# Reordering the first loads, tile 3's transposes and PE's idle matmuls in a fused linear attention and SwiGLU kernel

## The chip, the cores and the metric

The kernel runs on one core of a Trainium2 chip. The metric is the device time of one execution in microseconds (us). The engines are called as in the profile: PE (TensorE, matmuls; PEld is its weight load), DVE (VectorE), ACT (ScalarE), POOL (GpSimd) and SP (SyncE, which here only issues DMAs). ACT issues DMAs too. Each engine works through its own list of instructions in program order.

## The reference

`x` is 2048 x 512, in bf16, as are all weights.

```python
def phi(t): return where(t > 0, t + 1, exp(t)) + 1e-6

xn = layernorm(x)                       # over the last axis, no scale or shift
q, k, v = split(xn @ wqkv)              # 32 heads of 16
kv  = einsum("bhsd,bhse->bhde", phi(k), v)
z   = phi(k).sum over s
o   = (phi(q) @ kv) / (phi(q) . z + 1e-6)
A   = o @ wo
B   = (silu(xn @ w_gate) * (xn @ w_up)) @ w_down     # 512 -> 1792 -> 512
out = x + A + B
```

## The kernel before

`x` is cut into 16 tiles of 128 rows; tile t lies in `x_sb[:, t, :]` with one row in each partition. The program is written out by hand as calls like `stat(4)` or `kproj(2)`. Each call appends instructions to the lists of the engines that it uses. A small class `_Prog` remembers who wrote and who reads each named resource (`("x", t)`, `("xnT", t)`, `("bank", i)`, ...) and adds the semaphore waits. So the order of calls is the order of work on every engine, and an instruction that waits holds up all that stands behind it on its engine. A DMA that waits holds up its issuing engine's queue in the same way.

The steps of a tile t are:

- `stat(t)`: mean and variance on DVE (`bn_stats`, L275; `bn_aggr`, L278), then the reciprocal root of the variance on POOL (L294, L301). For tile 0 the addition of 1e-5 (L294) is on DVE.
- `xn(t)` or `xn_dve(t)`: the normalized tile `xn_sb`, on DVE (L283). Tile 0 is done in two halves of columns (`xn_half`, L326).
- The transpose of `xn_sb` into `xnT`: for tiles 0 to 2 four matmuls against an identity on PE and a copy out of PSUM on ACT (`transpose_half` L338 and L347, `transpose_pe` L310 and L317), for later tiles a DMA on SP's queue (`transpose_dma`, L354).
- `kproj(t)` and `qproj(t)`: four matmuls of 512 columns each (L363; `proj_half` L376 for K of tile 0), into PSUM banks `kb(t)` = 0 or 2 and `qb(t)` = 1 or 3.
- `exp_k(t)` and `exp_q(t)` on ACT (L399, L405, L409), then `feat_k(t)` on DVE (clip L416, maximum and addition L425), which also puts the running sum of phi(k) on POOL (`zsum`, L446 and L450).
- `gtacc(t)`: four matmuls (L458) that add the transpose of xn times phi(k) into banks 4 to 7, over all tiles. Until then the transposes on PE use banks 4 to 7.

After the 16 tiles comes a long part in which PE is fed from `xnT`: the FFN's gate and up matmuls (`ffn_mm`, L550), the small matrices of the attention (L648, L671), and the output tiles (L722, L733, with the addition of `x` at L746). This part is the same before and after.

The first loads are issued on two queues, SP's and ACT's: x tiles, then the columns of `wqkv` for K ("wk") and for Q ("wq"), each in two parts of 256 KB, one on each queue (`wqkv_load`, L202). x tiles 4 to 15 are loaded by SP in four DMAs, of which the first waits for x 0 and x 1 (`xload`, L195). `fill` (L247) puts matmuls without use for the result on PE while it has no other work. They multiply a tile of zeros, `idle`, which DVE sets at the start (L241).

In the loop over tiles, tables give which later tiles get their `stat` (STAT) and their `xn` (XN) in iteration t, and `wpiece` issues the parts of `w_gate` and `w_up` on SP's queue.

Of the kernel before, what the change touches and what calls it, by code (L numbers as in the profile page):

```python
# [10 lines left out]
P = 128  # L11
# [3 lines left out]
NT = S // P  # L15
# [93 lines left out]
def bass_parallel_sum__linear_attn_block__swiglu_ffn__prompt_kernel(  # L109
# [12 lines left out]
    K = _Prog()  # L122
    pe, act, dve, pool, sp = nc.tensor, nc.scalar, nc.vector, nc.gpsimd, nc.sync
    bf, f32 = dt.bfloat16, dt.float32

    with contextlib.ExitStack() as es:
        E = es.enter_context

        def sb(name, shape, d=bf):
            return E(nc.sbuf_tensor(name, [P] + shape, d))  # L130

        x_sb = sb("x_sb", [NT, D])
# [4 lines left out]
        wg_sb = sb("wg_sb", [NDC, F])  # L137
# [5 lines left out]
        stats = sb("stats", [NT, 6], f32)  # L143
        mv = sb("mv", [NT, 2], f32)
        vpe = sb("vpe", [NT], f32)
        rstd = sb("rstd", [NT], f32)
# [2 lines left out]
        ek = sb("ek", [NE, D])  # L149
        eq = sb("eq", [NT, D])  # L150
        warm = sb("warm", [1], f32)
        idle = sb("idle", [512])
        pkq = sb("pkq", [NT, 2, D])
        zacc = sb("zacc", [D], f32)
        zhi = sb("zhi", [D])
# [19 lines left out]
        banks = [psum[:, i, :] for i in range(8)]  # L175
# [10 lines left out]
        def bk(i):  # L186
            return ("bank", i)


        xv = xin.rearrange("(p t) d -> p t d", t=NT)  # L190
        ov = oview.rearrange("(p t) d -> p t d", t=NT)

        def xload(eng, h, t0, n, after=()):
            K.dma(
                eng, lambda: h.dma_start(x_sb[:, t0:t0 + n, :], xv[:, t0:t0 + n, :]),  # L195
                r=list(after), w=[("x", t0 + i) for i in range(n)],
            )

        def wqkv_load(eng, h, name, i, c0, n):
            K.dma(  # L200
                eng,
                lambda: h.dma_start(  # L202
                    wqkv_sb[:, c0:c0 + n, i * D:(i + 1) * D],
                    A_wqkv[c0 * P:(c0 + n) * P, i * D:(i + 1) * D].rearrange("(c p) f -> p c f", p=P),
                ),
                w=[(name, c0)],
            )
# [4 lines left out]
        def wpiece(name, dst, src, c):  # L212
            K.dma("sp", lambda: sp.dma_start(dst[:, c, :], src[c * P:(c + 1) * P, :]), w=[(name, c)])

        xload("sp", sp, 0, 1)
        xload("act", act, 1, 1)
        wqkv_load("sp", sp, "wk", 1, 0, 2)
        wqkv_load("act", act, "wk", 1, 2, 2)
        xload("sp", sp, 2, 1)
        xload("act", act, 3, 1)  # L220
        wqkv_load("sp", sp, "wq", 0, 0, 2)
        wqkv_load("act", act, "wq", 0, 2, 2)
        xload("sp", sp, 4, 2, [("x", 0), ("x", 1)])
        xload("sp", sp, 6, 4)
        xload("sp", sp, 10, 2)
        xload("sp", sp, 12, 4)

# [10 lines left out]
            r=[("ident",)], w=[("ident",)],  # L238
        )
        K.op("pool", lambda: pool.memset(nhalf[:, :], -0.5), w=[("nhalf",)])  # L240
        K.op("dve", lambda: dve.memset(idle[:, :], 0.0), w=[("idle",)])  # L241

        def fill(n, after):
            K.op(
                "pe",
                [
                    (lambda: pe.matmul(banks[3], idle[:, 0:P], idle[:, :], start=True, stop=True))  # L247
                    for _ in range(n)
                ],
                r=[("idle",)] + after, w=[bk(3)],  # L250
            )

        def masks():
# [18 lines left out]


        def bns(t):
            K.op("dve", lambda: dve.bn_stats(stats[:, t, :], x_sb[:, t, :]), r=[("x", t)], w=[("st", t)])  # L275

        def agg(t):
            K.op("dve", lambda: dve.bn_aggr(mv[:, t, :], stats[:, t, :]), r=[("st", t)], w=[("mv", t)])  # L278
# [1 line left out]
        def xn_dve(t):  # L280
            K.op(
                "dve",
                lambda: dve.tensor_scalar(  # L283
                    out=xn_sb[:, t, :], in0=x_sb[:, t, :], scalar1=mv[:, t, 0:1], scalar2=rstd[:, t:t + 1],
                    op0=ALU.subtract, op1=ALU.mult,
                ),
                r=[("x", t), ("mv", t), ("rstd", t)], w=[("xn", t)],
            )
# [16 lines left out]
        def transpose_pe(t, b):  # L305
            tb = banks[b].bitcast(bf)[:, 0:512].rearrange("p (c s) -> p c s", c=NDC)
            K.op(
                "pe",
                [
                    (lambda c=c: pe.transpose(tb[:, c, :], xn_sb[:, t, c * P:(c + 1) * P], ident[:, :]))  # L310
                    for c in range(NDC)
                ],
                r=[("xn", t), ("ident",)], w=[bk(b)],
            )
            K.op(
                "act",
                lambda: act.activation(xnT[:, :, t * P:(t + 1) * P], tb, ACT.Copy),  # L317
                r=[bk(b)], w=[("xnT", t)],
            )
# [52 lines left out]
        def proj_half(t, b, lo, wname, h):  # L372
            K.op(
                "pe",
                [
                    (lambda c=c: pe.matmul(  # L376
                        banks[b], xnT[:, c, t * P:(t + 1) * P], wqkv_sb[:, c, lo:lo + D],
                        start=(c == 0), stop=(c == NDC - 1),
                    ))
                    for c in (2 * h, 2 * h + 1)  # L380
                ],
                r=[("xnTh", t, h), (wname, 2 * h)], w=[bk(b)],
            )

        def kb(t):
            return 2 * (t % 2)
# [4 lines left out]
        def kproj(t):  # L391
            proj(t, kb(t), D, "wk")

        def qproj(t):
            proj(t, qb(t), 0, "wq")

        def exp_k(t):
            K.op(
                "act", lambda: act.activation(ek[:, t % NE, :], banks[kb(t)], ACT.Exp),  # L399
                r=[bk(kb(t))], w=[("ek", t % NE)],  # L400
            )

        def exp_q(t):
            K.op(
                "act", lambda: act.activation(eq[:, t, :], banks[qb(t)], ACT.Exp),  # L405
                r=[bk(qb(t))], w=[("eq", t)],
            )
            K.op(
                "act", lambda: act.activation(pkq[:, t, 1, :], banks[qb(t)], ACT.Copy),  # L409
                r=[bk(qb(t))], w=[("pq", t)],  # L410
            )
# [19 lines left out]
        def feat_k(t):  # L431
            e = t % NE
            clip(ek[:, e, :], ("ek", e))
            if t >= 1:
                zsum(t - 1, e)
            maxadd(pkq[:, t, 0, :], banks[kb(t)], ek[:, e, :], [bk(kb(t)), ("ek", e)], [("pk", t)])
# [17 lines left out]
        def gtacc(t):  # L454
            K.op(
                "pe",
                [
                    (lambda c=c: pe.matmul(  # L458
                        banks[4 + c], xn_sb[:, t, c * P:(c + 1) * P], pkq[:, t, 0, :],
                        start=(t == 0), stop=(t == NT - 1),  # L460
                    ))
                    for c in range(NDC)
                ],
                r=[("xn", t), ("pk", t)], w=[bk(4 + c) for c in range(NDC)],
            )

        def stat(t):
            bns(t)
            agg(t)
            rstd_pow(t)  # L470

        def xn(t):
            xn_dve(t)
            if t >= 3:
                transpose_dma(t)

        stat(0)
        stat(1)
        xn_half(0, 0)
        xn_half(0, 1)  # L480
        xn_dve(1)
        stat(2)
        stat(3)
        xn_dve(2)

        fill(10, [])
        fill(1, [("mv", 0)])
        fill(1, [("rstd", 0)])
        transpose_half(0, 4, 0)
        transpose_half(0, 5, 1)  # L490
        fill(1, [])
        proj_half(0, kb(0), D, "wk", 0)
        proj_half(0, kb(0), D, "wk", 1)
        exp_k(0)
        transpose_pe(1, 6)
        qproj(0)
        exp_q(0)
        transpose_pe(2, 7)
        kproj(1)
        qproj(1)  # L500
        feat_k(0)
        xn(3)

        STAT = {0: (4, 5), 1: (6,), 2: (7,), 3: (8,), 4: (9, 10), 5: (11,), 6: (12,), 7: (13,), 8: (14, 15)}
        XN = {0: (4,), 1: (5,), 2: (6,), 3: (7,), 4: (8,), 5: (9, 10), 6: (11,), 7: (12,), 8: (13,), 9: (14, 15)}

        for t in range(NT):
            if t >= 2:
                kproj(t)
            if t >= 1:  # L510
                exp_k(t)
            if t >= 2:
                qproj(t)
            if t >= 1:
                exp_q(t)
                feat_k(t)
            for i in STAT.get(t, ()):
                stat(i)
            for i in XN.get(t, ()):
                xn(i)  # L520
            if t in (2, 4, 6, 8):
                wpiece("wg", wg_sb, B_w_gate, t // 2 - 1)
            if t == 11:
                for c in range(NDC):
                    wpiece("wu", wu_sb, B_w_up, c)
                wqkv_load("sp", sp, "wv", 2, 0, 4)
                wload("sp", sp, "wo", wo_sb, A_wo)
            if t == 14:
                wload("sp", sp, "wd", wd_sb, B_w_down)
            if t == 12:  # L530
                masks()
            if t >= 2:
                gtacc(t - 2)
        zsum(NT - 1, None)
        gtacc(NT - 2)
# [292 lines left out]
```

## Time and profile before

| | |
|---|---|
| runs | 214.15, 214.5, 215.22 us; median 214.5 |
| the profiled execution | 214.34 us |
| its span (first to last instruction) | 213.0 us |
| PE busy | 207.5 us, 97% of the span |
| DVE, ACT, POOL busy | 119.4, 67.6 and 72.6 us |
| granted TensorE clock, mean of the span | 1.00 |
| a matmul of 512 columns behind another, from 10 us on | 0.216 us |
| FFN's first matmul (L550) in the chain of waits | 49.94 us |

Times in the profile are microseconds from the first instruction. The execution's time is 1.34 us longer than its span. In the timeline a row gives the start, the busy time, engine, line, operation, output and inputs, the count, and in brackets how long the engine sat idle before it and what released it. The duration of one matmul record is its latency (379 ns for 512 columns in a dense stretch); matmuls overlap, so the distance between their starts is what PE needs for one. The granted clock of the page is 1.00 throughout, also in the first microseconds, in which matmuls of 512 columns follow one another at 0.43 us.

### The profile page before, as it was taken

How to read it: one execution, taken by the hardware profiler on the slowest of the kernel's cores; microseconds unless marked ns; L12 is line 12 of the kernel's file. 1: busy time of each engine (PE TensorE's matmuls, PEld its weight loads, DVE VectorE, ACT ScalarE, POOL GpSimd, SP SyncE). 2: the span in 40 equal slices, each digit the busy share in tenths (PEclk: the TensorE clock that was granted, in tenths of full speed). 3: DMA queues.
4: the chain of work that ended last, by engine and by line, in shares of the span. 5: the costliest groups of instructions: out<-in, count | busy, mean ns of one | idle time of the engine just before them, and what ended most of it. 6: DMA issues, size and time to landing. Idle time of an engine off the chain costs nothing.

```text
span 213.0 us, 2744 instructions
## 1 busy us (share of the span) xinstructions
PE 207.5 (97%) x972; PEld 96.0 (45%) x991; DVE 119.4 (56%) x241; ACT 67.6 (32%) x117; POOL 72.6 (34%) x95
## 2 busy tenths in 40 slices
PE   7899999999999999999999999999999999999995
PEld 2344444444544444444444444444444444444454
DVE  2899997333544776446373746464556536364121
ACT  2576666667353332213122302112032213121000
POOL 1559996646013444032130442131414131221100
PEclk9999999999999999999999999999999999999999
DMA  5924598899102011110101011101011010110201
GB/s 188 388 65 125 139 143 207 287 368 266 26 0 52 0 25 25 49 24 28 31 20 49 3 35 39 49 0 49 3 49 25 25 25 28 49 25 26 51 28 51
DMA packets 26671, 16.32 MB, mean 77 GB/s; under 512 B 18592, under 2 KB 25120, under 8 KB 26656
## 3 DMA queue, kind: packets, MB, share of 16 engines
q1 hardware_dynamic: 25824, 15.34, 27.1%
q10 hardware_dynamic: 832, 0.79, 1.2%
q8 instruction: 8, 0.13, 0.3%
q14 instruction: 7, 0.06, 0.1%
HBM read 9.70 MB, written 2.10 MB: 55 GB/s over the span
## 4 chain that ended last, share of the span: by engine, by line
PE 94%; DVE 2%; DMA 2%; issue 1%; POOL 1%; DVEq 0%
PE psum L550 45%; PE psum L733 23%; PE psum L363 12%; PE psum L722 6%; PE psum L458 6%; DMA x_sb<-in_A_x_dram 2%; DVE stats L275 1%; POOL rstd L301 1%; PE psum L648 0%; PE psum L671 0%; DVE xn_sb L283 0%; DVE mv L278 0%; POOL vpe L294 0%; DVE out_sb L746 0%; PE psum L310 0%
## 5 line engine op out<-in xcount | busy, mean ns | idle before, releaser
L565 ACT ACTIVATE sg<-psum 128x512 bf16<-128x512 f32 x56 | 33.4, 598 | 106.8 <-PE psum L550 106.0
L550 PE MATMUL psum<-xnT,wu_sb 128*128 128x512 bf16 x222 | 57.4, 379 | 0.1
L550 PE MATMUL psum<-xnT,wg_sb 128*128 128x512 bf16 x217 | 56.0, 379 | 0.4
L680 POOL TENSOR_TENSOR prod<-pkq,zb 128x512 f32<-128x512 bf16 x16 | 18.6, 1161 | 57.8 <-DVE pkq L425 57.8
L550 PEld LDWEIGHTS psum<-xnT,wu_sb 128*128 128x128 bf16 x224 | 21.9, 98 | 26.4
L550 PEld LDWEIGHTS psum<-xnT,wg_sb 128*128 128x128 bf16 x224 | 21.9, 98 | 26.2
L746 DVE TENSOR_TENSOR out_sb<-psum,x_sb 128x512 bf16<-128x512 f32 (+1 forms) x17 | 11.2, 660 | 36.1 <-PE psum L733 36.1
L571 DVE TENSOR_TENSOR pkq<-psum,sg 128x512 bf16<-128x512 f32 x28 | 19.1, 686 | 18.6 <-PE psum L550 14.1
L704 POOL TENSOR_TENSOR pqn<-pkq,rden 128x512 bf16<-128x512 bf16 x16 | 16.9, 1055 | 36.6 <-DVE rden L698 36.6
L363 PE MATMUL psum<-wqkv_sb,xnT 128*128 128x512 bf16 x122 | 29.0, 379 | 0.3
L571 DVE TENSOR_TENSOR xn_sb<-psum,sg 128x512 bf16<-128x512 f32 x28 | 18.8, 671 | 14.2 <-PE psum L550 13.6
L733 PE MATMUL psum<-wd_sb,xn_sb 128*128 128x512 bf16 (+1 forms) x124 | 25.6, 355 | 0.1
L733 PE MATMUL psum<-wd_sb,pkq 128*128 128x512 bf16 x110 | 25.4, 379 | 0.1
L450 POOL TENSOR_TENSOR zacc<-zacc,pkq 128x512 f32<-128x512 f32 x15 | 17.3, 1153 | 6.9 <-DVE ek L416 6.8
L363 PEld LDWEIGHTS psum<-wqkv_sb,xnT 128*128 128x128 bf16 x124 | 12.0, 98 | 14.5 <-DMA wqkv_sb<-in_A_wqkv_dram 0.3
L733 PEld LDWEIGHTS psum<-wd_sb,xn_sb 128*128 128x128 bf16 x126 | 12.3, 98 | 11.9
L733 PEld LDWEIGHTS psum<-wd_sb,pkq 128*128 128x128 bf16 x112 | 11.0, 98 | 13.2
L722 PE MATMUL psum<-m_sb,eq 128*128 128x512 bf16 (+1 forms) x66 | 16.2, 366 | 0.1
L458 PE MATMUL psum<-pkq,xn_sb 128*128 128x512 bf16 x62 | 15.8, 379 | 0.1
L688 DVE TENSOR_REDUCE den<-prod 128x32 f32<-128x512 f32 x16 | 10.9, 683 | 5.7 <-POOL prod L680 5.7
L399 ACT ACTIVATE ek<-psum 128x512 bf16<-128x512 f32 x16 | 9.6, 598 | 9.9 <-DVE ek L416 2.8
L275 DVE BATCH_NORM_STATS2 stats<-x_sb 128x6 f32<-128x512 bf16 x16 | 10.9, 679 | 2.9 <-DMA x_sb<-in_A_x_dram 2.9
(57 smaller groups left out, 128.4 us busy)
## 6 DMA issues: line engine op xcount, KB each, us to landing
out_dram<-out_sb SPq DMA_DIRECT2D x15, 128.0 KB, 1.7
wg_sb<-in_B_w_gate_dram SPq DMA_DIRECT2D x4, 448.0 KB, 3.8
wu_sb<-in_B_w_up_dram SPq DMA_DIRECT2D x4, 448.0 KB, 4.8
wd_sb<-in_B_w_down_dram SPq DMA_DIRECT2D x1, 1792.0 KB, 13.6
x_sb<-in_A_x_dram SPq DMA_DIRECT2D x2, 512.0 KB, 6.4
wqkv_sb<-in_A_wqkv_dram ACTq DMA_DIRECT2D x2, 256.0 KB, 4.9
wqkv_sb<-in_A_wqkv_dram SPq DMA_DIRECT2D x2, 256.0 KB, 5.2
x_sb<-in_A_x_dram SPq DMA_DIRECT2D x2, 256.0 KB, 5.6
```

Of the source, the lines that this page charges most:

```text
L275: K.op("dve", lambda: dve.bn_stats(stats[:, t, :], x_sb[:, t, :]), r=[("x", t)], w=[("st", t)])
L363: (lambda c=c: pe.matmul(banks[b], xnT[:, c, t * P:(t + 1) * P], wqkv_sb[:, c, lo:lo + D], start=(c == 0), stop=(c == NDC - 1),))
L450: lambda: pool.tensor_tensor(out=zacc[:, :], in0=zacc[:, :], in1=pk, op=ALU.add),
L458: (lambda c=c: pe.matmul(banks[4 + c], xn_sb[:, t, c * P:(c + 1) * P], pkq[:, t, 0, :], start=(t == 0), stop=(t == NT - 1),))
L550: (lambda c=c: pe.matmul(banks[b], w_sb[:, c, fc * P:(fc + 1) * P], xnT[:, c, C * 512:(C + 1) * 512], start=(c == 0), stop=(c == NDC - 1),))
L565: lambda: act.activation(sg[:, j % NSG, :], banks[gb], ACT.Silu),
L571: lambda: dve.tensor_tensor(out=hT(C, fc), in0=banks[ub], in1=sg[:, j % NSG, :], op=ALU.mult,),
L680: lambda: pool.tensor_tensor(out=p, in0=pkq[:, t, 1, :], in1=zb[:, :], op=ALU.mult),
L704: lambda: pool.tensor_tensor(out=pqn[:, t % NPN, :].rearrange("p (h e) -> p h e", e=DH), in0=pkq[:, t, 1, :].rearrange("p (h e) -> p h e", ...
L722: (lambda g=g: pe.matmul(dst, pqnT(t)[:, g, :], m_sb[:, g, lo:hi], start=(g == 0), stop=False,))
L733: (lambda fc=fc: pe.matmul(dst, hT(C, fc)[:, jj * P:(jj + 1) * P], wd_sb[:, fc, lo:hi], start=False, stop=(fc == NFC - 1),))
L746: lambda: dve.tensor_tensor(out=o, in0=src, in1=x_sb[:, t, lo:hi], op=ALU.add),
```

## The change

- x tiles 0 and 1 are loaded in two parts of 64 rows each, one on each queue; both queues start with tile 0.
- x 2 stays on SP between wk and wq. On ACT, wq's part now goes ahead of x 3. x 4 and 5 wait for both parts of wk (instead of x 0 and 1), x 6 to 9 for both parts of wq; x 10 to 15 follow on the same queue.
- Tile 3 is transposed on PE (bank 4) instead of by a DMA. `kproj(1)` goes ahead of tile 2's transposes, `exp_k(0)` behind tile 1's, and tiles 2 and 3 are written out with their own order of `stat`, `xn`, `feat_k` and `gtacc`.
- In the loop a tile's `xn` stands ahead of the next `stat`, both tables change, and the four parts of `w_gate` are issued in iterations 5, 7, 9 and 10 instead of 2, 4, 6 and 8.
- The idle matmuls read constants of 1.0 that the program holds anyway, so DVE's memset goes. They no longer wait for anything; ten have 512 columns and six have 128.

```diff
-        idle = sb("idle", [512])
...
-        xload("sp", sp, 0, 1)
-        xload("act", act, 1, 1)
+        def xpart(eng, h, t, p0):
+            K.dma(
+                eng, lambda: h.dma_start(x_sb[p0:p0 + P // 2, t, :], xv[p0:p0 + P // 2, t, :]),
+                w=[("xp", t, p0)] + ([("x", t)] if p0 else []),
+            )
+
+        for t in (0, 1):
+            xpart("sp", sp, t, 0)
+            xpart("act", act, t, P // 2)
         wqkv_load("sp", sp, "wk", 1, 0, 2)
         wqkv_load("act", act, "wk", 1, 2, 2)
         xload("sp", sp, 2, 1)
+        wqkv_load("act", act, "wq", 0, 2, 2)
+        wqkv_load("sp", sp, "wq", 0, 0, 2)
         xload("act", act, 3, 1)
-        wqkv_load("sp", sp, "wq", 0, 0, 2)
-        wqkv_load("act", act, "wq", 0, 2, 2)
-        xload("sp", sp, 4, 2, [("x", 0), ("x", 1)])
-        xload("sp", sp, 6, 4)
+        xload("sp", sp, 4, 2, [("wk", 0), ("wk", 2)])
+        xload("sp", sp, 6, 4, [("wq", 0), ("wq", 2)])
         xload("sp", sp, 10, 2)
         xload("sp", sp, 12, 4)
...
-        K.op("dve", lambda: dve.memset(idle[:, :], 0.0), w=[("idle",)])
-
-        def fill(n, after):
+        cw = nc.const_aps.tensor(1.0, (P, P), bf)
+        cx = nc.const_aps.tensor(1.0, (P, 512), bf)
+
+        def fill(n, cols):
             K.op(
                 "pe",
                 [
-                    (lambda: pe.matmul(banks[3], idle[:, 0:P], idle[:, :], start=True, stop=True))
+                    (lambda: pe.matmul(banks[3][:, 0:cols], cw, cx[:, 0:cols], start=True, stop=True))
                     for _ in range(n)
                 ],
-                r=[("idle",)] + after, w=[bk(3)],
+                w=[bk(3)],
             )
...
         def xn(t):
             xn_dve(t)
-            if t >= 3:
+            if t >= 4:
                 transpose_dma(t)
 
         stat(0)
         stat(1)
         xn_half(0, 0)
         xn_half(0, 1)
-        xn_dve(1)
+        xn(1)
         stat(2)
         stat(3)
-        xn_dve(2)
-
-        fill(10, [])
-        fill(1, [("mv", 0)])
-        fill(1, [("rstd", 0)])
+        xn(2)
+
+        fill(10, 512)
+        fill(4, P)
         transpose_half(0, 4, 0)
         transpose_half(0, 5, 1)
-        fill(1, [])
+        fill(2, P)
         proj_half(0, kb(0), D, "wk", 0)
         proj_half(0, kb(0), D, "wk", 1)
+        transpose_pe(1, 6)
         exp_k(0)
-        transpose_pe(1, 6)
         qproj(0)
         exp_q(0)
+        kproj(1)
         transpose_pe(2, 7)
-        kproj(1)
         qproj(1)
+        exp_k(1)
+        exp_q(1)
         feat_k(0)
+        stat(4)
         xn(3)
...
+        kproj(2)
+        transpose_pe(3, 4)
+        qproj(2)
+        exp_k(2)
+        exp_q(2)
+        feat_k(1)
+        xn(4)
+        stat(5)
+        gtacc(0)
+
+        XN = {2: (5,), 3: (6,), 4: (7,), 5: (8,), 6: (9,), 7: (10, 11), 8: (12,), 9: (13,), 10: (14, 15)}
+        STAT = {2: (6,), 3: (7,), 4: (8,), 5: (9,), 6: (10, 11), 7: (12,), 8: (13,), 9: (14, 15)}
+        WG = {5: 0, 7: 1, 9: 2, 10: 3}
+
+        for t in range(2, NT):
+            if t >= 3:
                 kproj(t)
...
                 exp_k(t)
...
                 qproj(t)
...
                 exp_q(t)
...
+            feat_k(t)
+            for i in XN.get(t, ()):
+                xn(i)
             for i in STAT.get(t, ()):
                 stat(i)
...
+            if t in WG:
+                wpiece("wg", wg_sb, B_w_gate, WG[t])
...
-            if t >= 2:
+            if t >= 3:
                 gtacc(t - 2)
```

More of the change, by code (lines that the diff above doesn't have):

```diff
@@ L274, in bns @@
         def bns(t):
-            K.op("dve", lambda: dve.bn_stats(stats[:, t, :], x_sb[:, t, :]), r=[("x", t)], w=[("st", t)])
+            K.op("dve", lambda: dve.bn_stats(stats[:, t, :], x_sb[:, t, :]),
+                 r=[("x", t)] + ([("xp", t, 0)] if t < 2 else []), w=[("st", t)])
         def agg(t):
@@ L480, in bass_parallel_sum__linear_attn_block__swiglu_ffn__prompt_kernel @@
         xn_half(0, 1)
-        xn_dve(1)
+        xn(1)
         stat(2)
         stat(3)
-        xn_dve(2)
-        fill(10, [])
-        fill(1, [("mv", 0)])
-        fill(1, [("rstd", 0)])
+        xn(2)
+        fill(10, 512)
+        fill(4, P)
         transpose_half(0, 4, 0)
         transpose_half(0, 5, 1)
-        fill(1, [])
+        fill(2, P)
         proj_half(0, kb(0), D, "wk", 0)
         proj_half(0, kb(0), D, "wk", 1)
+        transpose_pe(1, 6)
         exp_k(0)
-        transpose_pe(1, 6)
         qproj(0)
         exp_q(0)
+        kproj(1)
         transpose_pe(2, 7)
-        kproj(1)
         qproj(1)
+        exp_k(1)
+        exp_q(1)
         feat_k(0)
+        stat(4)
         xn(3)
-        STAT = {0: (4, 5), 1: (6,), 2: (7,), 3: (8,), 4: (9, 10), 5: (11,), 6: (12,), 7: (13,), 8: (14, 15)}
-        XN = {0: (4,), 1: (5,), 2: (6,), 3: (7,), 4: (8,), 5: (9, 10), 6: (11,), 7: (12,), 8: (13,), 9: (14, 15)}
-        for t in range(NT):
-            if t >= 2:
+        kproj(2)
[12 more added lines that the diff above has]
+            if t >= 3:
                 kproj(t)
-            if t >= 1:
                 exp_k(t)
-            if t >= 2:
                 qproj(t)
-            if t >= 1:
                 exp_q(t)
-                feat_k(t)
+            feat_k(t)
+            for i in XN.get(t, ()):
+                xn(i)
             for i in STAT.get(t, ()):
                 stat(i)
[L519 to L522, printed above, removed]
+            if t in WG:
+                wpiece("wg", wg_sb, B_w_gate, WG[t])
             if t == 11:
@@ L531, in bass_parallel_sum__linear_attn_block__swiglu_ffn__prompt_kernel @@
                 masks()
-            if t >= 2:
+            if t >= 3:
                 gtacc(t - 2)
```

## The prediction

> **What bounds the kernel now.** I read the page first, then the chain of waits, then the timeline of the first 14 us. The page gives PE 97% of the span and the chain gives it 94%, so only a moment at which PE has no real work can be shortened. The chain, in order of time (start, length, what), shows where those moments are:
>
> ```profile
> 0.80 3.31 DMA x_sb<-in_A_x_dram
> 4.13 0.70 DVE stats L275
> ...
> 6.45 0.59 POOL rstd L301
> ...
> 8.76 0.58 POOL rstd L301
> 10.23 3.45 PE psum L363 x16
> 13.74 0.81 PE psum L458 x3
> 14.55 1.73 PE psum L363 x8
> ```
>
> Up to about 10 us the chain hops between a transfer, DVE and POOL; afterwards it is PE alone, 8 projections in 1.73 us and 4 accumulations in 0.86, so 0.216 us for a matmul of 512 columns. After 10.07 PE has 120 projection matmuls and 64 of L458 before the FFN: 184 x 0.2157 = 39.7 us, which ends at 49.8, and the chain has the FFN (L550) start at 49.94. Nothing is to be had there, nor in the FFN. The change must earn its time before 10.07. PE's own timeline of that stretch (start, length, form, count, idle time and releaser):
>
> ```profile
> 7.97 0.39 PE L310 MATMUL psum<-ident,xn_sb 128*128 128x128 bf16 x4
> 8.51 1.04 PE L363 MATMUL psum<-wqkv_sb,xnT 128*128 128x512 bf16 x4
> 9.83 0.40 PE L310 MATMUL psum<-ident,xn_sb 128*128 128x128 bf16 x4 [0.29 <-DVE xn_sb L283]
> 10.07 0.38 PE L363 MATMUL psum<-wqkv_sb,xnT 128*128 128x512 bf16 x1
> 8.51 0.55 PEld L363 LDWEIGHTS psum<-wqkv_sb,xnT 128*128 128x128 bf16 x4 [0.32 <-DMA wqkv_sb<-in_A_wqkv_dram]
> ```
>
> Two holes: PE is free at 8.19 and waits 0.32 us for wq; then qproj(0) issues until 8.51 + 4 x 0.216 = 9.37, and tile 2's transposes start only at 9.83, 0.46 us later, because xn(2) is late on DVE. Four transposes cost 0.24 us (9.83 to 10.07). Ahead of 8.19 PE stands at the end of a chain that begins with x 0. Landings of the first loads by queue, issue plus time to landing: x 0 (SP) 0.80 + 3.3 = 4.10, x 1 (ACT) 3.9, wk 5.1 (ACT) and 5.5 (SP), x 3 6.8, x 2 7.05, wq 8.0 (ACT) and, the line of SP's part:
>
> ```profile
> L202 SPq DMA_DIRECT2D wqkv_sb<-in_A_wqkv_dram x1: 439/439/439, 2.3 to 2.3; - x1
> DMA to landing us min/median/max: 6.2/6.2/6.2
> ```
>
> 2.29 + 6.2 = 8.49. That row, not the arithmetic, releases qproj(0).
>
> **The change part by part.** Call s the start of qproj(0), 8.51 now. From s on, before: 0.86 + 0.46 hole + 0.24 + 39.7. After: kproj(1) goes between qproj(0) and tile 2's transposes and needs only tile 1, so the hole is covered by 0.86 us of work; tile 3's transposes move from SP's queue to PE, +0.24. Gain = (8.51 - s) + 0.46 - 0.24 - new waits.
>
> *x 0 and 1 in halves.* By the windows of 0.2 us the DMA engines start at 1.85 and have moved 131 KB by 2.5 and 262 KB by 3.15; x 0 and x 1 land 0.75 and 0.95 after the latter. With both queues on x 0 first, its 131 KB are through by 2.5 and land at 3.25 to 3.45: at most 0.85 earlier. At least nothing: the time to landing may be all latency. I take 0.6, nearer the byte count, because the two landings now follow the bytes by under 1 us. x 1 needs its issue (0.40) behind x 0's, and lands near 3.9 as now; bn_stats of tile 1 would start at 5.15 - 0.6 = 4.55, so it doesn't wait. Everything from bn_stats(0) through xn_half, transposes, ACT's copies and proj_half (0.69, 0.18, 0.15, 0.55 and on) moves together: PE is ready for qproj(0) at 8.19 - 0.6 = 7.6. wk is one issue (0.4) later, near 5.9 against a need at 6.5: covered. ACT's table load is pushed from 2.71 to 3.1 and ends at 4.6, before its first copy at 6.1: covered.
>
> The Trainium skill speaks against the halves: "DMA: Bandwidth & Descriptors", section Bandwidth, calls transfers under 64 KB descriptor-dominated, and these are 64 KB each; the fit in its Anatomy section, made for the GpSimd path, would make 131 KB 2.30 us and 64 KB 2.15, an estimate of 0.15 us gained instead of 0.6. By it the total would be the same, since wq and not x would then still be what PE waits for.
>
> *wq.* Its SP part has the same bytes ahead of it in its queue (64 + 64 + 256 + 128 KB), one issue more (0.40 to 0.50 by the rows): up to 0.4 later, 8.9. On the other side, x 4 to 9 are no longer issued at 4.1 but behind wk's and wq's landings. By the windows the engines had moved 1.57 MB at 7.0, exactly x 0 to 3, wk and wq, but wq landed at 8.5 with 2.0 MB moved at 8.0: other transfers went between. Without them 7.0 + 0.75 to 0.95 gives 7.8 to 8.0. Bounds 7.8 and 8.9; I take 8.2, near ACT's part (8.0). PE, ready at 7.6, waits until then, so s = 8.25 and x's gain itself is mostly hidden behind wq.
>
> *x 3 and DVE.* x 3 moves behind wq on ACT, so it lands with wq, 8.2 instead of 6.8. stat(3) stands ahead of xn(2) in DVE's queue: 8.2 + 0.85 (bn_stats and aggregate, 8.29 to 9.1 now) + 0.1 + 0.41 = 9.6 for xn(2). PE asks for it at s + 1.73 = 9.98. Covered by 0.4; each 0.1 us that x 3 lands beyond s + 0.35 costs 0.1.
>
> *New waits.* x 4 waits on SP for wk, x 6 for wq; behind them queue x 10, x 12 and the first DMA transpose (tile 4, near 13). x 4 lands near 9.3 (9.12 now) and is read at 10.6; x 6 to 15 land up to 1 us later and are read from 15 on. stat(4) stands ahead of xn(3), whose transposes PE reaches near 12.0; by DVE's durations xn(3) is done at 11.9. kproj(2) needs ACT's copy of tile 2 (ready 11.1 against 11.1), gtacc(0) needs the copy of tile 3 out of bank 4 (13.2 against 13.1). Together 0.1 us, from 0 to 0.4. feat_k(1) now comes before xn(4), which relieves the DVE that was busy 96% and more from 13 to 18 us. Tiles from 5 on are normalized one tile later relative to kproj: xn(5) near 15.5, a DMA transpose lands 2.4 to 3.3 us after issue (up to 4.4 later on), kproj(5) near 19.3. Covered. wg's pieces and wu's keep some 10 us to the FFN.
>
> *Fills.* The memset on DVE (0.92, 0.27 us) goes, so PE's idle matmuls start at about 0.95 instead of 1.25; the three of 512 columns between the transposes become six of 128. They lie beside waits, and cost nothing unless the clock changes. What they hold up is the clock: PE's loads of weights for the fills start at 2.08, 2.51, 2.93, 3.36, so 0.43 us a matmul; the rows of the idle tile then go from 634 ns to 379 between 4.2 and 5.0, and the pitch becomes 0.216. So 3.6 us of steady matmuls came before full speed. From 0.95 this gives 4.55, and the fills end between 5.0 and 5.65, tile 0's transposes start at 5.74. I take full speed there, cost 0.
>
> *Sum.* (8.51 - 8.25) + 0.46 - 0.24 - 0.1 = 0.38 us. The profiled execution took 214.34 us (span 213.0 and 1.34 around it), 0.16 below the median of the runs shown. 214.34 - 0.38 = 213.95, which I leave uncorrected.
>
> **The rivals.** *All early:* wq at 7.8 or below, x 0 0.85 earlier and no new waits. Then s = 7.5 to 7.8 and the gain is 0.71 + 0.22 = 0.9 to 1.2, so 213.1 to 213.4. For it: 1.57 MB moved at 7.0. Against: 8.49 was reached with the same bytes ahead.
>
> *The order of loads does not do what it says:* wq lands at 8.9 by its later issue, x 3 at 9.3 with it, both edits of the queues then bring nothing. Gain (8.51 - 8.95) + 0.22 - 0.1 = -0.3: 214.65. For it: SP's part is moved to a later place in time and to no other place in its queue.
>
> *The clock, slower than before:* PE is empty from the end of the fills (5.0 to 5.65) to 5.74, and from there to 7.5 it has 0.24 us of transposes, 0.11 of fills and 0.86 of projections where it had 0.6 us of fills as well. If that is too little to reach or keep full speed when qproj(0) starts, PE needs up to 3.6 us more of steady work at 0.43: 8.4 matmuls x 0.21 = 1.8 us at most, half if it comes halfway. 213.95 + 0.9 to 1.8 = 214.9 to 215.7. It decides if the release, seen 3.6 us after the first fill, comes later than 5.0 to 5.65. For it: one execution shows the release only once. Against: between 5.6 and 6.7 PE has pauses of 0.33 us and short work now, and keeps 379 ns. The skill's page "TensorE: Matmul & The Clock Gate", Part 1, says that the window of about 3.4 us runs freely and does not start with the kernel; by it, an estimate, one window more at half speed would cost 1.7 us, 215.6.
>
> **How the numbers follow.** Forecast, own range 213.4 to 214.4: 0.50. All early: 0.24. Loads no earlier: 0.11. Clock: 0.15. A difference of 0.5%, 1.07 us, is about what a measurement of this kernel can tell from no change (its three runs lie 1.07 apart). Faster by more takes nearly all of the second case (0.22) and 0.04 from the lower edge of the first: 0.26. Slower: the clock and a little of the third, 0.16. The rest, 0.58, is within. The range goes from 212.9 (below the best of the second case, for the runs' scatter) to 215.4, which leaves out half of the clock's case and a little of the second.
>
> **What would show it.** Right: bn_stats(0) at 3.5, qproj(0) at 8.0 to 8.4, kproj(1) directly behind it, no idle time of PE over 0.15 us between qproj(0) and 14 us, FFN start at 49.5. Wrong in the loads: wq's SP part landing over 8.7, or PE waiting for xn(2) with x 3 as its cause. Wrong in the clock: matmul records of 634 ns behind tile 0's transposes. Wrong altogether: PE waiting for a DMA transpose between 16 and 30 us, or an FFN start that moves while the total doesn't.

## The result: slower, and the profile after

The changed kernel takes 217.9 us in the median (217.45 to 218.68) against 214.5 before: 1.0156 of the time, interval 1.0129 to 1.0183, 3.4 us more. The forecast was 213.95 us with a range up to 215.4, so both the sign and the range were wrong. The profiled execution took 218.68 us (span 217.4), 0.8 us above the median; its late start, shown further down, is the likely reason.

The head of the page (span; busy time, share and instructions of each engine):

```profile
span 217.4 us, 2761 instructions
...
PE 209.6 (96%) x979; PEld 96.7 (44%) x998; DVE 126.2 (58%) x240; ACT 67.9 (31%) x118; POOL 72.0 (33%) x95
```

DVE has one instruction fewer than before and 6.8 us more busy time (119.4 before). The chain of waits, which before was PE alone from 10 us on, now runs through DVE and POOL until past 40 us (start, length, what):

```profile
23.50 0.61 DVE stats L283
...
24.14 0.19 DVE mv L287
...
24.40 0.23 POOL vpe L303
...
24.71 0.58 POOL rstd L310
...
25.31 1.23 DVE xn_sb L292
26.55 0.61 DVE stats L283
...
54.60 3.45 PE psum L568 x16
```

One round, from bn_stats to bn_stats, is 3.05 us, and PE needs 2.59 for a tile. The FFN (L568) starts at 54.60 instead of 49.94; from there to the end of the span it is 162.8 us against 163.1 before. All the loss lies ahead of the FFN. The step that has grown is xn (L292), whose row over all tiles (minimum, median, maximum in ns) reads

```profile
L292 DVE TENSOR_SCALAR xn_sb<-x_sb,mv,rstd x15: 381/1234/1249, 7.2 to 42.4; 128x512 bf16<-128x512 bf16 x15
```

where the kernel before had 379/411/1356. The timelines of DVE and POOL show what is beside it. After:

```profile
24.53 0.69 DVE L434 SCALAR_TENSOR_TENSOR pkq<-psum,ek 128x512 bf16<-128x512 f32 x1
25.31 1.23 DVE L292 TENSOR_SCALAR xn_sb<-x_sb,mv,rstd 128x512 bf16<-128x512 bf16 x1
26.47 0.68 DVE L283 BATCH_NORM_STATS2 stats<-x_sb 128x6 f32<-128x512 bf16 x1
...
24.71 0.57 POOL L310 TENSOR_TENSOR rstd<-vpe,nhalf 128x1 f32<-128x1 f32 x1
25.24 1.15 POOL L459 TENSOR_TENSOR zacc<-zacc,pkq 128x512 f32<-128x512 f32 x1
```

and the same work in the kernel before:

```profile
17.69 0.69 DVE L425 SCALAR_TENSOR_TENSOR pkq<-psum,ek 128x512 bf16<-128x512 f32 x1
18.29 0.69 DVE L275 BATCH_NORM_STATS2 stats<-x_sb 128x6 f32<-128x512 bf16 x1
19.01 0.18 DVE L278 BATCH_NORM_AGGREGATE mv<-stats 128x2 f32<-128x6 f32 x1
19.11 0.50 DVE L283 TENSOR_SCALAR xn_sb<-x_sb,mv,rstd 128x512 bf16<-128x512 bf16 x1
...
17.77 0.57 POOL L301 TENSOR_TENSOR rstd<-vpe,nhalf 128x1 f32<-128x1 f32 x1
18.31 1.15 POOL L450 TENSOR_TENSOR zacc<-zacc,pkq 128x512 f32<-128x512 f32 x1
```

After, xn starts at 25.31 and ends at 26.54; POOL's running sum of phi(k) runs from 25.24 to 26.39. The two begin together, 0.06 to 0.07 us apart, in every round with a single tile, and not by chance: xn of a tile now waits for the root (`rstd`) that POOL has just computed, and the sum stands directly behind that root in POOL's queue, so the end of the root releases both. (In the two rounds with a pair of tiles the second xn of the pair meets the sum.) Before, `stat` stood between the maximum and xn, and the sum ran beside bn_stats, 0.69 us with or without it; only its last 0.35 us met xn, which took 0.50.

The Trainium skill has this as a rule, which I did not weigh: "SBUF — State Buffer", section Who interferes with whom, says that DVE and GpSimd share a pair of ports under an exclusive lock held for a whole instruction, and names tensor_scalar among the operations that can take it. The trace agrees in that xn ends 0.15 us behind the sum, before and after, and that bn_stats is untouched. 0.15 us is less than the 0.38 that xn takes alone, so a part of its own time passes beside the sum; which part, and whether xn moves nothing meanwhile, can't be read from it.

### The profile page after: what moved, and what is told of

It is laid out like the page before. It is cut to its first block, busy times and chain, and to the rows that moved or that the text cites. A ratio compares the mean times of both kernels' runs of the same rounds, so it can differ in the third digit from the quotient of the medians.

```text
span 217.4 us, 2761 instructions
## 1 busy us (share of the span) xinstructions
PE 209.6 (96%) x979; PEld 96.7 (44%) x998; DVE 126.2 (58%) x240; ACT 67.9 (31%) x118; POOL 72.0 (33%) x95
## 4 chain that ended last, share of the span: by engine, by line
PE 81%; DVE 11%; POOL 3%; DMA 2%; issue 1%; ACT 1%; ACTq 0%; DVEq 0%
PE psum L568 44%; PE psum L751 22%; PE psum L740 6%; DVE xn_sb L292 5%; PE psum L372 4%; DVE stats L283 3%; PE psum L467 2%; POOL rstd L310 2%; DMA x_sb<-in_A_x_dram 2%; DVE pkq L434 1%; DVE mv L287 1%; PE psum L385 1%; POOL vpe L303 1%; PE psum L666 0%; PE psum L689 0%
## 5 line engine op out<-in xcount | busy, mean ns | idle before, releaser
L568 PE MATMUL psum<-xnT,wu_sb 128*128 128x512 bf16 x222 | 57.4, 379 | 0.1
L568 PE MATMUL psum<-xnT,wg_sb 128*128 128x512 bf16 x217 | 56.0, 379 | 0.4
L568 PEld LDWEIGHTS psum<-xnT,wu_sb 128*128 128x128 bf16 x224 | 21.9, 98 | 26.4 <-issue 0.2
L568 PEld LDWEIGHTS psum<-xnT,wg_sb 128*128 128x128 bf16 x224 | 21.9, 98 | 26.2
L751 PEld LDWEIGHTS psum<-wd_sb,xn_sb 128*128 128x128 bf16 x126 | 12.3, 98 | 11.9
L292 DVE TENSOR_SCALAR xn_sb<-x_sb,mv,rstd 128x512 bf16<-128x512 bf16 x15 | 13.4, 908 | 1.2 <-POOL rstd L310 0.6
```

What stands on the lines that cost most here:

```text
L292: lambda: dve.tensor_scalar(out=xn_sb[:, t, :], in0=x_sb[:, t, :], scalar1=mv[:, t, 0:1], scalar2=rstd[:, t:t + 1], op0=ALU.subtract, op1= ...
L568: (lambda c=c: pe.matmul(banks[b], w_sb[:, c, fc * P:(fc + 1) * P], xnT[:, c, C * 512:(C + 1) * 512], start=(c == 0), stop=(c == NDC - 1),))
L751: (lambda fc=fc: pe.matmul(dst, hT(C, fc)[:, jj * P:(jj + 1) * P], wd_sb[:, fc, lo:hi], start=False, stop=(fc == NFC - 1),))
```

## The experiments

The first three tell the cause of the 3.4 us, the next ones what the rest of the change is worth. Ratios are to the kernel before.

**stat ahead of xn again** (the changed kernel otherwise):

```diff
-        xn(4)
         stat(5)
+        xn(4)
...
-            for i in XN.get(t, ()):
-                xn(i)
             for i in STAT.get(t, ()):
                 stat(i)
+            for i in XN.get(t, ()):
+                xn(i)
```

> The changed kernel with stat ahead of xn again in the loop and for tile 4; loads, fills and tables as changed. Theory A (xn directly behind feat_k starts together with POOL's running sum and stands until it ends): xn is back at 0.4 to 0.5 us from 1.23, the DVE round of a tile goes from 3.05 to about 2.2 us, PE is the bound again from 14.4 us on; 168 matmuls of 0.2157 are left there, so the FFN starts near 50.7 and the time is 213.9 to 214.3 us. Rival B (the tables, tiles normalized one iteration later): the round stays over 2.59 and the time at 217 to 218. Rival C (late loads of x 4 to 15): same as B, with DVE waiting for a transfer.

Measured: 214.36 us, 0.9985 (0.9960 to 1.0011), so 3.5 us less than the changed kernel and just above the 213.9 to 214.3 expected. The FFN starts at 50.34 instead of 54.60. xn's row:

```profile
L292 DVE TENSOR_SCALAR xn_sb<-x_sb,mv,rstd x15: 380/383/1316, 6.6 to 37.1; 128x512 bf16<-128x512 bf16 x15
```

Loads, fills and tables are those of the change; rivals B and C fall as the cause of the loss.

**The kernel before with xn ahead of stat**, the opposite edit. Tile 4 is left out of it, since its xn would come before its own mean and variance:

```diff
-            for i in STAT.get(t, ()):
-                stat(i)
-            for i in XN.get(t, ()):
-                xn(i)
+            if t == 0:
+                stat(4)
+                stat(5)
+                xn(4)
+            else:
+                for i in XN.get(t, ()):
+                    xn(i)
+                for i in STAT.get(t, ()):
+                    stat(i)
```

> The kernel before with one edit: xn ahead of stat in the loop (tile 4 keeps stat ahead of xn, which it needs). Theory A: xn at about 1.2 us in the iterations that also have the running sum, a DVE round of 2.9 to 3.05 us, FFN start at 52.5 to 54.5, 216.5 to 218.5 us. Rivals B and C (the tables or the loads were what mattered): no change, 214.2 to 214.8.

Measured: 218.67 us, 1.0194 (1.0177 to 1.0211). FFN start 54.34. Nothing but this order was changed, and it costs 4.25 us, more than the whole change does.

```profile
L283 DVE TENSOR_SCALAR xn_sb<-x_sb,mv,rstd x15: 403/1232/1246, 7.2 to 39.6; 128x512 bf16<-128x512 bf16 x15
```

**Without the running sum** (the changed kernel; the sum of phi(k) is left out for tiles 1 to 14):

```diff
-            if t >= 1:
+            if t == 1:
                 zsum(t - 1, e)
```

> The changed kernel without POOL's running sum of phi(k) for tiles 1 to 14 (it is left out; nothing else). Theory A: xn 0.38 to 0.42 us although it still stands ahead of stat, 213.9 to 214.3 us. Rival D (xn is slow because it follows the maximum, or because its input comes late, not because of POOL): xn stays at 1.2 and the time at 217 to 218.

Measured: 213.99 us, 0.9971 (0.9954 to 0.9988). xn keeps its new place directly behind the maximum, and is fast there:

```profile
L292 DVE TENSOR_SCALAR xn_sb<-x_sb,mv,rstd x15: 381/412/507, 6.4 to 35.9; 128x512 bf16<-128x512 bf16 x15
```

The FFN starts at 50.01. So it is POOL's sum beside xn, not xn's place. By the chain's own terms the round would be 3.05 - 1.23 + 0.41 = 2.23 us without the overlap, under PE's 2.59.

**The new order of tiles 0 to 3 alone**: the first experiment with the loads and the fills of the kernel before.

> As e1_stat_first, but with the loads and the fills of the kernel before: what is left of the change is tile 3 on PE and the new order of tiles 0 to 3. By the prediction's own terms, the hole of 0.46 us closed, 0.24 us of transposes added, 0.1 of new waits: FFN start at 49.8 and 214.1 to 214.4 us. If the new loads and fills cost what the changed kernel's trace shows before 14 us (PE at half speed until 9.6 us, x 1 landing at 5.1 instead of 3.9), e1_stat_first is 0.5 to 1 us slower than this one; if the new start is worth its 0.26 us, e1_stat_first is that much faster.

Measured: 213.62 us, 0.9957 (0.9939 to 0.9975), better than the 214.1 to 214.4 expected; and once more:

> e4_schedule_only once more, with more rounds, as the base for the three kernels sent with it: 0.995 to 0.997 of before, 213.4 to 213.8 us.

Measured: 213.64 us, 0.9960 (0.9946 to 0.9973). The chain of the second one has

```profile
49.67 3.45 PE psum L561 x16
```

0.27 us before the old 49.94. With qproj(0) at 8.47 the prediction's sum gives (8.51 - 8.47) + 0.46 - 0.24 = 0.26. The medians differ by 0.9; the traces show the 0.27 and 0.3 at the end of the span, behind the last instruction on DVE, and the rest stays open.

**Loads and fills apart**, on the same schedule. New loads, old fills:

> Schedule of e4_schedule_only, loads as changed, fills as before. With e1_stat_first (both new, 0.9985 of before) and e4_schedule_only (both old, 0.9957) this tells which of the two costs the 0.74 us between them. Theory L (the loads: parts of 64 rows take 0.57 to 0.87 us to issue instead of 0.4, wq lands no earlier, x 6 to 15 come later): 214.2 to 214.5, like e1_stat_first. Theory F (the fills, by a later release of the clock): 213.5 to 213.7, like e4_schedule_only.

Measured: 214.02 us, 0.9983 (0.9962 to 1.0004). Old loads, new fills:

> Schedule of e4_schedule_only, loads as before, fills as changed. Theory L: 213.5 to 213.7. Theory F: 214.2 to 214.5, with matmul records of 634 ns behind tile 0's transposes in some executions and a wider scatter of the times.

Measured: 213.69 us, 0.9966 (0.9939 to 0.9994). The fills make no difference that these intervals can tell; the loads lean to the slow side, but not clear of the schedule alone either. Both have a wider scatter (up to 215.0 and 215.75) than the schedule alone.

**The loads apart.** Halves of x 0 and x 1 only, all else of the loads as before:

```diff
-        xload("sp", sp, 0, 1)
-        xload("act", act, 1, 1)
+        for t in (0, 1):
+            xpart("sp", sp, t, 0)
+            xpart("act", act, t, P // 2)
```

> The base with x 0 and x 1 in parts of 64 rows, the order and the waits of all other loads as before. Theory L1 (it is the parts that cost: their issue of 0.57 to 0.87 us delays wk, x 2, x 3 and wq by about 0.9 us at issue): x 0 lands near 3.4, wq at 8.2 to 8.9, 0.3 to 0.6 us over the base. Theory L2 (the order costs, by x 3 and x 4 to 15 coming late): equal to the base within 0.2 us.

Measured: 214.77 us, 1.0010 (0.9993 to 1.0026), where the schedule alone in the same comparison has 0.9960 (0.9946 to 0.9973): 1.1 us lost. The queue of ACT and PE's timeline in this run:

```profile
0.81 1.47 ACTq L217 DMA_DIRECT2D x_sb<-in_A_x_dram  x2
...
3.47 0.46 ACTq L202 DMA_DIRECT2D wqkv_sb<-in_A_wqkv_dram  x1
...
9.34 1.89 PE L372 MATMUL psum<-wqkv_sb,xnT 128*128 128x512 bf16 x8 [1.44 <-DMA wqkv_sb<-in_A_wqkv_dram]
```

Two half loads keep ACT's queue for 1.47 us (0.56 and 0.88 one by one) and SP's for 1.21, where one whole load took 0.39 to 0.40. wq's ACT part is issued at 3.47 instead of 2.22, lands 5.7 us later at 9.2, and PE, ready early, stands 1.44 us for it. That is more than the 0.3 to 0.6 us and the 8.2 to 8.9 expected. Only the order of loads, with whole tiles:

> The base with whole x 0 and x 1 and only the new order: wq ahead of x 3 on ACT, x 4 and 6 waiting for wk and wq. Theory L1: equal to the base or up to 0.3 us better, wq landing at 7.5 to 8.0. Theory L2: 0.3 to 0.6 us over the base, with DVE waiting for x 3 or PE for a DMA transpose.

Measured: 213.9 us, 0.9967 (0.9954 to 0.9981), not to be told from the schedule alone. Theory L1 holds: the parts cost. In the changed kernel wq goes ahead of x 3 on ACT (issued at 2.7 to 3.0, landing at 7.3 to 7.6, with SP's part at 8.1 to 8.7). Parts and order together give 0.9983, between the two. That the order gives part of the loss back fits these landings, but it is not shown: the interval of 0.9983 overlaps those of both the halves alone and the schedule alone.

**The tables one tile earlier:**

```diff
-        XN = {2: (5,), 3: (6,), 4: (7,), 5: (8,), 6: (9,), 7: (10, 11), 8: (12,), 9: (13,), 10: (14, 15)}
+        XN = {2: (5, 6), 3: (7,), 4: (8,), 5: (9,), 6: (10,), 7: (11, 12), 8: (13,), 9: (14, 15)}
```

> e4_schedule_only with the table of xn one tile earlier from tile 6 on (as in the kernel before), stat still ahead of xn. In e4_schedule_only PE loses about 0.4 us between 13.8 and the FFN start (49.15 by 164 matmuls of 0.2157, 49.60 measured) and waits before projections at 16.35 and 26.96. If late DMA transposes cause it, FFN start at 49.2 and 213.1 to 213.4 us; if not, 213.5 to 213.8.

Measured: 217.93 us, 1.0159 (1.0143 to 1.0176), a miss of mine. With `stat(i)` and `xn(i)` in one iteration, DVE computes the variance and then waits for POOL's root of it:

```profile
25.31 0.18 DVE L279 BATCH_NORM_AGGREGATE mv<-stats 128x2 f32<-128x6 f32 x1
26.56 0.41 DVE L284 TENSOR_SCALAR xn_sb<-x_sb,mv,rstd 128x512 bf16<-128x512 bf16 x1 [1.07 <-POOL rstd L302]
```

It is a second way to the same loss: DVE's round is 3.2 us, though xn itself takes 0.41. Then the pair of tiles moved to an early iteration, with `stat` one iteration ahead of its xn throughout:

```diff
-        XN = {2: (5,), 3: (6,), 4: (7,), 5: (8,), 6: (9,), 7: (10, 11), 8: (12,), 9: (13,), 10: (14, 15)}
-        STAT = {2: (6,), 3: (7,), 4: (8,), 5: (9,), 6: (10, 11), 7: (12,), 8: (13,), 9: (14, 15)}
+        XN = {2: (5,), 3: (6,), 4: (7, 8), 5: (9,), 6: (10,), 7: (11,), 8: (12,), 9: (13,), 10: (14, 15)}
+        STAT = {2: (6,), 3: (7, 8), 4: (9,), 5: (10,), 6: (11,), 7: (12,), 8: (13,), 9: (14, 15)}
```

> The base with the two tiles in one iteration moved from iterations 6 and 7 to 3 and 4, stat always one iteration ahead of its xn (which e7_tables_earlier did not keep: there DVE waited 1.07 us for POOL's root in each iteration). DMA transposes from tile 8 on get one iteration more to land. If they cause the 0.4 us that PE loses between 13.8 and the FFN start: FFN start at 49.2 and 0.3 to 0.4 us under the base; if not, equal to it.

Measured: 213.5 us, 0.9953 (0.9937 to 0.9969); FFN start 49.54 instead of 49.67, not the 49.2 that late transposes as the cause would have given; where the 0.4 us go stays open. It is the fastest kernel here, but not to be told from the schedule alone. Both beat the kernel before (by 0.4 to 0.5%) and the changed one.

## Why the prediction was wrong, by its own steps

**The step that failed** is in "New waits": "by DVE's durations xn(3) is done at 11.9 [...] feat_k(1) now comes before xn(4), which relieves the DVE". It noticed that xn now stands directly behind feat_k and priced it at 0.41 us, or as a relief. It took the durations of DVE's rows as fixed, and never asked which of POOL's instructions would lie beside xn in its new place. In its sum this is the term of the new waits, put at 0.1 us (0 to 0.4); undoing the order alone won back 3.5 us. The price in the trace: 0.82 us a round (1.23 against 0.41), DVE's round 3.05 instead of 2.2, so 0.46 over PE's 2.59. Eight rounds lie between xn(5) and the last pair; at this price they make 3.7 us, an estimate, since rounds with a pair of tiles are longer. The old profile held a hint: xn's row had 379 ns at least and 1356 at most. Its 0.50 us fell exactly where the end of the sum overlapped it, and the 1356 is the one place in the old loop where xn had no `stat` between itself and the maximum (tile 14): it starts at 32.85, beside a sum that starts at 32.91. The rivals looked for the loss in the loads and in the clock, and so none of them held it.

**The closed hole and tile 3's transposes** were right. In the nine runs with the new schedule in which neither the sum nor the root holds up DVE's rounds, kproj(1) follows qproj(0) without a pause. The FFN starts 41.2 to 41.3 us behind qproj(0) in six of their traces (8.47 to 49.67 in the schedule alone, for one), where the sum 0.86 + 0.48 + 39.7 and the 0.18 lost in the old kernel give 41.2. In the other three it is 41.5 (schedule alone, 8.13 to 49.60), 41.9 (new fills, 8.12 to 50.06) and 42.1 (the first experiment, 8.22 to 50.34); for the last two see the DMA transposes below.

**x 0 in halves**: the size was right, the account was not. bn_stats(0) starts at 3.51 instead of 4.13, 0.62 earlier for 0.6 forecast. The fit on the Trainium skill's page "DMA: Bandwidth & Descriptors", section Anatomy of one DMA, made for the GpSimd path, would have given 0.15, an estimate; here the measurement decides against it. But the prediction priced the issue of a half at 0.4 us, that of a whole tile, and it is 0.57 to 0.87. So wk, x 2 and SP's part of wq are issued 0.8 to 1.1 us later and not 0.4, and x 1 may come late. The start of the changed kernel's profile:

```profile
5.18 0.69 DVE L283 BATCH_NORM_STATS2 stats<-x_sb 128x6 f32<-128x512 bf16 x1 [0.57 <-DMA x_sb<-in_A_x_dram]
...
7.25 1.89 PE L385 MATMUL psum<-wqkv_sb,xnT 128*128 128x512 bf16 x4
8.93 0.63 PE L319 MATMUL psum<-ident,xn_sb 128*128 128x128 bf16 x4
```

Tile 1's bn_stats waits 0.57 us for its half, which lands at 5.09 instead of the 3.9 forecast, and starts at 5.18, just as late as before (5.15); it stands ahead of xn_half(0) on DVE, and the whole gain of tile 0 is gone. In the first experiment x 1 came in time (4.56).

**wq** was expected at 8.2 between 7.8 and 8.9: it landed at 8.1 to 8.7 with halves and new order, within that range, but as the balance of a later issue than forecast and a shorter way to landing (4.9 to 5.2 us instead of 6.2). In the six other executions with the old loads the later of wq's two parts landed at 7.8 to 8.4, where the profile before had 8.49: that one row was at the late end of what it does.

**The clock**, a rival at 0.15, showed its sign in the profiled execution: tile 0's four projections have records of 609 to 634 ns and take 1.89 us, 0.43 apart, and the short distance comes only with the matmuls behind 9.8 us, though fills ran without a pause from 0.84 to 5.69. (The profile's own granted clock is 1.00 in each stretch of the first 14 us, so "clock" is here a name for the distance between matmuls; that a clock sets it is not shown.) In three others with the same fills (stat first, no sum, new fills) tile 0's projections take 1.02 to 1.04. Against the first experiment, the profiled one reaches gtacc(0) 1.4 us later (14.41 against 12.98), by this and by x 1. The chain of waits runs through it: from these projections it goes through ACT to tile 1's clip on DVE and on into the rounds of DVE and POOL, and that clip starts at 12.92, where the first experiment has 11.58. So this execution alone would have ended up to some 1.3 us earlier with the other's start, an estimate. That the new fills bring it about more often is not shown: the medians with old and new fills agree.

The 3.6 us of matmuls that the prediction allowed ahead of the short distance was a single reading. With the old fills, which begin at 1.25 us and have records of 634 ns from the second on, the first shorter one starts at 4.6 us in the kernel before, but at 3.8 in one other trace (order only), at 5.1 to 5.9 in six, and only at 6.8 in one (new loads). To take full speed at 5.74 as certain was more than one trace could show.

**DMA transposes** were called covered. In most executions they are, but the first experiment's shows an exception (SP's issue of tile 6's transpose with its time to landing, and PE):

```profile
L363 SPq DMA_TRANSPOSE xnT<-xn_sb x1: 1192/1192/1192, 18.1 to 18.1; - x1
DMA to landing us min/median/max: 4.4/4.4/4.4
...
22.55 1.89 PE L372 MATMUL psum<-wqkv_sb,xnT 128*128 128x512 bf16 x7 [0.77 <-ACT pkq L418]
```

The transposes around it landed in 2.4 to 2.5 us. This one lands at 22.5, and kproj(6), due at 21.6, starts at 22.55; the page puts the pause down to ACT's copy, which was long done. With the old tables xn(6) would have stood one iteration earlier. So the new tables can cost 0.8 us in an execution; how often they do was not measured by itself. The run with the new fills has a second case: tile 9's transpose, issued at 26.23, takes 3.7 us, and PE stands 0.53 us before 30.05. Why these transposes are slow, no run shows.

## What to carry to other kernels

When a change moves an instruction on one engine, price it with what the other engines will do at that moment, not only with its own duration: look which queue neighbour the same event releases, and look in the old profile for the one place where the two already meet. In this kernel POOL's sum of 1.15 us cost nothing beside bn_stats or the maximum that reads PSUM, and 0.82 us beside the bf16 tensor_scalar. Splitting a load to have its first part sooner cost issue time here that every later load on that queue paid; the last load that PE waited for decided, not the first.

## What the runs showed of the hardware

- A 128x512 bf16 tensor_scalar on DVE went from 0.38 to 0.41 us to 1.23 beside a 1.15 us addition on POOL and ended 0.15 us behind it; bn_stats (0.68 to 0.69) and the maximum with a PSUM input (0.69) kept their time beside it.
- A load of 64 rows of 1 KB took 0.55 to 0.88 us of its queue to issue, one of 128 rows 0.39 to 0.41 as the first on its queue and 0.45 to 0.53 as a later one. The half landed 2.3 to 2.6 us after issue where nothing was ahead of it, against 3.1 to 3.5 for the whole tile.
- Matmuls of 512 columns followed one another at 0.43 us at first and at 0.216 later. In nine traces with the same fills from 1.25 us on, the first record under the steady 634 ns started at 3.8 to 6.8 us; in the changed kernel's it came only near 9.8 us, after 4.85 us of matmuls without a pause and then work with pauses.
- A DMA transpose of 128x512 landed 2.4 us after issue as a rule, and 4.4 at most.
